# Turned attention tiles: mirrored by the fetch in place of the store

## The chip, the cores and the metric

The kernel runs on 1 core of one Trainium2 chip. The metric is the device time of one execution in microseconds (us); the three times of the kernel before are 1122.34, 1119.64 and 1121.96, their median is 1121.96 us.

## The reference, cut to what matters

```python
# 2 batches, S = 3136, D = 256, d_qk = 64, d_ff = 1024, float32
scores = (1 / S) * (z @ z.T)              # per batch, symmetric
attn   = maximum(scores, 0) ** 2          # symmetric too
x      = u * (attn @ v)
h      = maximum(x @ w_in, 0)
conv   = depthwise convolution of h over 3 neighbouring rows, conv_w
x      = (h * sigmoid(conv)) @ w_out
xn     = (x - mean) / sqrt(var + 1e-6) * g_ln
out    = x + maximum(xn @ w_ch1, 0) @ w_ch2
```

## The kernel before

**Tiling.** A batch's 3136 columns (queries) are cut into 7 chunks of 4, 4, 3, 4, 3, 3 and 4 tiles of 128, so a chunk is 512, 384 or (the last, with a half tile) 448 wide. Its rows (keys) are 25 tiles `j` of 128. For a chunk `c` and a tile `j` the kernel needs the squared scores `a`, 128 keys by the chunk's queries. `products` computes them: two matmuls, a Relu on ACT, a square on ACT or DVE. `scores` then splits `a` into a rounded part `ah` (ACT, sometimes DVE) and the rest `al` (DVE), and `av` adds six matmuls of both parts with `vh` and `vl` into PSUM.

**The mirror.** The matrix is symmetric, so a tile above the diagonal is the transpose of one below. For each tile whose keys belong to a later chunk, `spill` turns `a` on DVE (L624): the instruction transposes each block of 32 x 32 in its place, into a buffer `bl` (4 places). The blocks then still have to be exchanged. The kernel before does that in the store: four DMAs (two for the half tile), each of 32 partitions, write to the DRAM tensor `turned` in runs of 32 numbers, 128 bytes (L633). When the later chunk comes, `land` fetches its part of `turned` in one DMA, whole rows of 1.5 to 2 KB (L646), in place of the two matmuls and the square. There are 146 spills, 73 in each batch, mostly in the first chunks of a batch, and 154 fetches, mostly in the last ones. A fetch goes into one of the six places of `a`; at most four fetches hold places at once.

**The feed-forward blocks.** 17 blocks of 384 or 256 rows (`mlps`) run interleaved with attention, each when its chunks of `x` are through DRAM. Weights are loaded and decoded on DVE and ACT during the first chunks.

**Order.** All of this is a list of operations with the engines that may do them, prices (`PRICE`), due times and buffers. `Program.order` simulates the five queues (PE, ACT, DVE, POOL and SP, which issues every DMA) and emits the operations in the order of that simulation; each engine then runs its own queue in that order. A DMA books time of SP, and a transfer: `kb / RATE` in one shared pipe, then `LANDS`. Where the plan has a gap on PE, `fill` (L1128) puts matmuls of zeros. The old spill books 1.92 us of SP and `kb=w`, the old fetch 0.45 us and `kb=n/2`, for `w` or `n` columns.

Of the kernel before, what the change touches and what calls it, by code (L numbers as in the profile page):

```python
# [8 lines left out]
F32 = mybir.dt.float32  # L9
# [6 lines left out]
P = 128  # L16
NB, S, D, DQ, DFF = 2, 3136, 256, 64, 1024
# [5 lines left out]
TILES = [4, 4, 3, 4, 3, 3, 4]  # L23
SQ = 32
# [24 lines left out]


PRICE = {
    "mm": lambda n: 0.0087 + 0.000431 * n,
    "turn": lambda n: 0.109,
    "act": lambda n: 0.06 + 0.0009 * n,
    "pool_u32": lambda n: 0.2 + 0.0013 * n,
# [12 lines left out]
}  # L68

AFTER = {"PE": 0.2, "ACT": 0.165, "DVE": 0.15, "POOL": 0.13, "SP": 0.0}  # L70
RATE, LANDS = 300.0, 1.9
ENGINES = ("PE", "ACT", "DVE", "POOL", "SP")


# [15 lines left out]
class Program:  # L90
# [7 lines left out]
    def op(self, ways, fn, reads=(), writes=(), adds=(), takes=(), due=None, late=None, name="", port=False, kb=None):  # L98


        o = Op()
        o.ways, o.fn, o.due, o.late, o.name, o.port, o.kb = ways, fn, due, late, name, port, kb
        o.before, o.after, o.n = set(), [], len(self.ops)
        o.adds, o.spare = tuple(adds), None
        for k in reads:
            assert k in self.writers, (name, k)
            o.before.update(self.writers[k])
            self.readers.setdefault(k, []).append(o)
        for k in writes:
            o.before.update(self.writers.get(k, ()))  # L110
            o.before.update(self.readers.pop(k, ()))
            self.writers[k] = [o]
        for k in adds:
            o.before.update(self.readers.get(k, ()))
            self.writers.setdefault(k, []).append(o)
        o.before.discard(o)
        bufs = []
        for k in (*reads, *writes, *adds, *((t,) for t in takes)):
            if isinstance(k[0], Buf) and k[0] not in bufs:
                bufs.append(k[0])  # L120
        for b in bufs:
            b.users.append(o)
        o.bufs = bufs
        self.ops.append(o)
        return o
# [168 lines left out]
def attn_moe_kernel(ctx: ExitStack, tc: tile.TileContext, zt, ut, v, w_in, conv_w, w_out, g_ln, w1, w2, out):  # L294
    nc = tc.nc
# [9 lines left out]
    dram = ctx.enter_context(tc.tile_pool(name="dram", bufs=1, space=bass.MemoryType.DRAM))  # L305
# [63 lines left out]
    op = pr.op  # L369
    orders = {}  # L370

    def buf(tag, fixed=False, kind=None):
        if fixed:
            orders[tag] = orders.get(tag, 0) + 1
        return Buf(tag, orders[tag] if fixed else None, kind)

    def at(b, name=None):

        if b.ap is None:
            b.ap = tags[b.tag][1](name or b.tag)  # L380
        return b.ap
# [3 lines left out]
    def price(kind, n):  # L385
        return PRICE[kind](n)
# [213 lines left out]
    per = len(TILES)  # L600
    start_of = [sum(TILES[:i]) for i in range(per + 1)]
# [11 lines left out]
    turned = {}  # L613
    for c in range(NC):
        i = c % per
        rows = S - start_of[i + 1] * P
        if rows > 0:
            turned[c] = dram.tile([P * TILES[i], rows], F32, tag=f"turned{c}", name="turned")

    def spill(c, j, ab):  # L620
        w = chunks[c][1] - chunks[c][0]
        b = buf("bl")
        op(
            [("DVE", price("dve_turn", w))], lambda e: nc.vector.transpose(at(b, "bl")[:, :w], at(ab)[:, :w]),  # L624
            reads=[(ab, 0)], writes=[(b, 0)], name="bl", port=True,
        )
        k0 = (j - start_of[c % per + 1]) * P

        def write(e):
            blocks_ = at(b)[:, :w].rearrange("p (b k) -> p b k", k=SQ)  # L630
            for o in range(0, min(P, S - j * P), SQ):
                dst = turned[c][:, k0 + o : k0 + o + SQ].rearrange("(b q) k -> q b k", q=SQ)
                nc.sync.dma_start(out=dst, in_=blocks_[o : o + SQ])  # L633

        op([("SP", 1.92)], write, reads=[(b, 0)], writes=[("turned", c, j)], late=LANDS + w / RATE, kb=w, due=1e4, name="spill")

    def land(c, j):
        q0, q1 = chunks[c]
        n, i = q1 - q0, chunk_of[j]
        src = c - c % per + i  # L640
        k0 = (start_of[c % per] - start_of[i + 1]) * P
        r0 = (j - start_of[i]) * P
        b = buf("a", True, kind="ld")
        op(
            [("SP", 0.45)],
            lambda e: nc.sync.dma_start(out=at(b, "land")[:, :n], in_=turned[src][r0 : r0 + P, k0 : k0 + n]),  # L646
            late=LANDS + n / 2 / RATE, kb=n / 2, writes=[(b, 0)], name="land",
            reads=[("turned", src, jj) for jj in range(start_of[c % per], start_of[c % per + 1])],
        )
        return b  # L650

    def scores(c, j, due):
        q0, q1 = chunks[c]
        n = q1 - q0
        from_dram = mirrored(c, j)
        ab = land(c, j) if from_dram else buf("a", True)

        def a():
# [9 lines left out]
        if spilled(c, j):  # L668
            spill(c, j, ab)
# [468 lines left out]
    for o in order:  # L1138
# [8 lines left out]
        n = int((gaps.get(o, 0.0) - 0.1) / FILL)  # L1147
# [5 lines left out]
    for i in list(nc.cur_bb.bb.instructions):  # L1153
        e = str(i.engine)
# [47 lines left out]
```

## Time and profile before

| | |
|---|---|
| median of three times | 1121.96 us |
| span of the profiled execution (its own total isn't given) | 1119.3 us |
| PE busy | 1098.5 us (98%) |
| DVE busy | 857.9 us (77%) |
| ACT busy | 714.5 us (64%) |
| granted TensorE clock | 1.000 |
| DMA queue q1 | 326960 packets, 114.21 MB, 42.2% of 16 engines |
| packets under 512 bytes | 276528 |
| stores `turned<-bl` | 560 issues (372 of 64 KB, 188 of 48 KB) |
| fetches `land<-turned` | 154 issues (82 of 192 KB, 42 of 224 KB, 30 of 256 KB) |

A busy time is the union of an engine's instructions; matmuls are pipelined, so a busy PE may still be waiting inside. "SPq" is the queue of SP, whose issues aren't counted as busy. Releasers are inferred from semaphores.

### The profile page before, as it was taken

Reading aid. Unit: us, or ns where it says so; the run is one execution under the profiler, and the core shown is the slowest. Engines: PE = TensorE matmul, PEld = TensorE weight load, DVE = VectorE, ACT = ScalarE, POOL = GpSimd, SP = SyncE. Lnnn points to the kernel's source line nnn. Section 1 sums busy time; section 2 is a strip of 40 time slices with the busy share of each in tenths; the row PEclk is TensorE's granted clock in tenths of the full one; section 3 lists DMA queues with packets and bytes.
Section 4 is the critical chain, followed back from the end, with each engine's and each line's share of the span. In section 5 each row is a group of like instructions: output and inputs, shape, how many; then the busy total and the mean of one; then the engine's idle time right before and its main releaser. Section 6 shows DMA issues by size and latency. Waiting matters only on the chain.

```text
span 1119.3 us, 18987 instructions
## 1 busy us (share of the span) xinstructions
PE 1098.5 (98%) x6686; PEld 1028.0 (92%) x6686; DVE 857.9 (77%) x1810; ACT 714.5 (64%) x1473; POOL 30.4 (3%) x43
## 2 busy tenths in 40 slices
PE   9899999999999999999999999999999999999998
PEld 7777787899999989999999999999999999999998
DVE  7888889989869686868687778785857868477773
ACT  7668767786647576757665666664737647366552
POOL 2000000000000000000000000000000000000000
PEclk9999999999999999999999999999999999999999
DMA  7788877975444224253316242412433524220000
GB/s 199 149 199 157 198 148 181 225 179 175 96 126 134 76 64 81 43 90 83 70 44 109 83 78 63 103 50 51 90 109 92 146 65 122 76 82 27 25 15 19
DMA packets 327054, 115.41 MB, mean 103 GB/s; under 512 B 276528, under 2 KB 314800, under 8 KB 326960
## 3 DMA queue, kind: packets, MB, share of 16 engines
q1 hardware_dynamic: 326960, 114.21, 42.2%
q8 instruction: 52, 0.85, 0.3%
q14 instruction: 42, 0.34, 0.1%
HBM read 64.74 MB, written 46.47 MB: 99 GB/s over the span
## 4 chain that ended last, share of the span: by engine, by line
PE 85%; DVE 4%; DMA 4%; ACT 4%; issue 1%; SPq 1%; POOL 0%; DVEq 0%; ACTq 0%
PE av L739 10%; PE av L736 10%; PE av L738 10%; PE y L839 8%; PE y L837 8%; PE y L838 8%; PE h2ps L821 4%; PE h2ps L822 4%; PE h2ps L823 4%; PE hps L821 4%; PE hps L822 4%; PE hps L823 4%; PE s L694 3%; PE s L695 3%; DMA land<-turned 2%; DVE al L673 2%
## 5 line engine op out<-in xcount | busy, mean ns | idle before, releaser
L736 PE MATMUL av<-ah,vh 128*128 128x512 f32 (+2 forms) x700 | 258.5, 369 | 5.1 <-ACT ah L393 2.3
L739 PE MATMUL av<-ah,vl 128*128 128x512 f32 (+2 forms) x700 | 256.0, 366 | 0.0
L738 PE MATMUL av<-al,vh 128*128 128x384 f32 (+2 forms) x672 | 248.3, 370 | 6.6 <-DVE al L673 6.1
L1015 DVE SCALAR_TENSOR_TENSOR g2l<-h2ps,g2h 128x384 fp32r<-128x384 f32 (+1 forms) x136 | 73.2, 539 | 125.1 <-ACT g2h L1010 124.4
L1010 ACT ACTIVATE g2h<-h2ps 128x384 fp32r<-128x384 f32 (+1 forms) x136 | 65.1, 479 | 146.2 <-PE h2ps L823 145.5
L736 PEld LDWEIGHTS av<-ah,vh 128*128 128x128 f32 x700 | 131.7, 188 | 19.8 <-ACT ah L393 5.0
L738 PEld LDWEIGHTS av<-al,vh 128*128 128x128 f32 x672 | 126.4, 188 | 23.2 <-DVE al L673 13.2
L739 PEld LDWEIGHTS av<-ah,vl 128*128 128x128 f32 x700 | 131.6, 188 | 14.1
L703 ACT ACTIVATE a<-s 128x512 f32<-128x512 f32 (+2 forms) x196 | 105.9, 558 | 45.5 <-PE s L695 45.1
L673 DVE TENSOR_TENSOR al<-a,ah 128x512 fp32r<-128x512 f32 (+2 forms) x182 | 114.2, 637 | 9.2 <-ACT ah L393 8.5
L837 PE MATMUL y<-woh,gh 128*128 128x256 f32 x392 | 109.7, 280 | 0.7 <-DVE ysb L1023 0.7
L839 PE MATMUL y<-woh,gl 128*128 128x256 f32 x392 | 109.9, 280 | 0.3 <-DVE gl L903 0.3
L837 PE MATMUL y<-w2h,g2h 128*128 128x256 f32 x392 | 109.8, 280 | 0.2 <-DVE ysb L1023 0.2
L624 DVE STREAM_TRANSPOSE bl<-a 128x512 f32<-128x512 f32 (+1 forms) x146 | 95.0, 657 | 19.4 <-ACT a L712 9.9
L839 PE MATMUL y<-w2h,g2l 128*128 128x256 f32 x392 | 109.8, 280 | 0.0
L838 PE MATMUL y<-w2l,g2h 128*128 128x256 f32 x392 | 109.7, 280 | 0.0
L838 PE MATMUL y<-wol,gh 128*128 128x256 f32 x392 | 109.6, 280 | 0.0
L393 ACT CAST ah<-a 128x512 fp32r<-128x512 f32 (+2 forms) x185 | 105.8, 583 | 4.4 <-DVE a L708 3.2
L712 ACT ACTIVATE a<-a 128x512 f32<-128x512 f32 (+2 forms) x183 | 105.9, 593 | 1.4
L673 DVE TENSOR_TENSOR al<-land,ah 128x384 fp32r<-128x384 f32 (+2 forms) x154 | 90.3, 595 | 16.5 <-ACT ah L393 15.8
L863 ACT ACTIVATE t<-h,cw 128x384 f32<-128x384 f32 (+1 forms) x136 | 81.9, 605 | 27.8 <-DVE gl L903 26.6
L393 ACT CAST ah<-land 128x384 fp32r<-128x384 f32 (+2 forms) x146 | 78.5, 547 | 31.5 <-DMA land<-turned 22.4
(119 smaller groups left out, 2442.9 us busy)
## 6 DMA issues: line engine op xcount, KB each, us to landing
turned<-bl SPq DMA_DIRECT2D x372, 64.0 KB, 1.9
land<-turned SPq DMA_DIRECT2D x82, 192.0 KB, 3.1
land<-turned SPq DMA_DIRECT2D x42, 224.0 KB, 3.9
turned<-bl SPq DMA_DIRECT2D x188, 48.0 KB, 1.8
land<-turned SPq DMA_DIRECT2D x30, 256.0 KB, 3.4
out_dram<-ysb SPq DMA_DIRECT2D x15, 384.0 KB, 2.8
vst<-in_v_dram SPq DMA_DIRECT2D x11, 512.0 KB, 4.0
x<-gated SPq DMA_DIRECT2D x14, 386.0 KB, 3.8
```

The costliest lines, as they stand in the source:

```text
L393: nc.scalar.copy(dst, src)
L624: [("DVE", price("dve_turn", w))], lambda e: nc.vector.transpose(at(b, "bl")[:, :w], at(ab)[:, :w]),
L673: lambda e: nc.vector.tensor_tensor(at(al, "al")[:, :n], a(), f(at(ah)[:, :n]), ALU.subtract),
L703: [("ACT", price("act_ps", n))], lambda e: nc.scalar.activation(a(), at(ps)[:, :n], AF.Relu),
L712: op([("ACT", price("act", n))], lambda e: nc.scalar.activation(a(), a(), AF.Square), writes=[(ab, 0)], name="square")
L736: nc.tensor.matmul(p, vhj, at(ah)[:, :n], start=first(b, d), stop=False, **kw)
L738: nc.tensor.matmul(p, vhj, at(al)[:, :n], start=False, stop=False, **kw)
L739: nc.tensor.matmul(p, vlj, at(ah)[:, :n], start=False, stop=False, **kw)
L821: nc.tensor.matmul(p, a, h_, start=d == 0, stop=False)
L837: nc.tensor.matmul(p, a, wh, start=first(acc, (i0 + i) // 2), stop=False, **kw)
L838: nc.tensor.matmul(p, a, wl, start=False, stop=False, **kw)
L839: nc.tensor.matmul(p, b, wh, start=False, stop=k == NF - 1, **kw)
```

## The change

The store writes `bl` as it stands, 128 partitions in one DMA, to a tensor of another shape: one plane of 128 columns for each tile of the chunk, in runs of 128 numbers (512 bytes). The fetch exchanges the blocks: four DMAs, each to 32 partitions, in runs of 32 numbers (128 bytes). The planner's prices of both follow, so do `LANDS` (1.9 to 1.6) and the price of a matmul, and all orders are planned anew with them. Number and shapes of the operations on PE, ACT, DVE and POOL stay, but for the fillers.

```diff
-    "mm": lambda n: 0.0087 + 0.000431 * n,
+    "mm": lambda n: 0.0022 + 0.000449 * n,
...
-RATE, LANDS = 300.0, 1.9
+RATE, LANDS = 300.0, 1.6
+SPILL_KB, LAND_KB = 0.53, 0.91
...
-        rows = S - start_of[i + 1] * P
-        if rows > 0:
-            turned[c] = dram.tile([P * TILES[i], rows], F32, tag=f"turned{c}", name="turned")
+        later = sum(TILES[i + 1 :])
+        if later > 0:
+            turned[c] = dram.tile([TILES[i], later * P, P], F32, tag=f"turned{c}", name="turned")
...
-        k0 = (j - start_of[c % per + 1]) * P
+        r0 = (j - start_of[c % per + 1]) * P
+        rows = min(P, S - j * P)
         def write(e):
-            blocks_ = at(b)[:, :w].rearrange("p (b k) -> p b k", k=SQ)
-            for o in range(0, min(P, S - j * P), SQ):
-                dst = turned[c][:, k0 + o : k0 + o + SQ].rearrange("(b q) k -> q b k", q=SQ)
-                nc.sync.dma_start(out=dst, in_=blocks_[o : o + SQ])
-        op([("SP", 1.92)], write, reads=[(b, 0)], writes=[("turned", c, j)], late=LANDS + w / RATE, kb=w, due=1e4, name="spill")
+            dst = turned[c][:, r0 : r0 + rows, :].rearrange("t p x -> p t x")
+            nc.sync.dma_start(out=dst, in_=at(b)[:rows, :w].rearrange("p (t x) -> p t x", x=P))
+        op(
+            [("SP", 0.4)], write, reads=[(b, 0)], writes=[("turned", c, j)],
+            late=LANDS + SPILL_KB * w / RATE, kb=SPILL_KB * w, due=1e4, name="spill",
+        )
...
-        k0 = (start_of[c % per] - start_of[i + 1]) * P
-        r0 = (j - start_of[i]) * P
+        g0 = (start_of[c % per] - start_of[i + 1]) * (P // SQ)
         b = buf("a", True, kind="ld")
-        op(
-            [("SP", 0.45)],
-            lambda e: nc.sync.dma_start(out=at(b, "land")[:, :n], in_=turned[src][r0 : r0 + P, k0 : k0 + n]),
-            late=LANDS + n / 2 / RATE, kb=n / 2, writes=[(b, 0)], name="land",
+        def read(e):
+            blocks_ = turned[src][j - start_of[i]].rearrange("(g q) (b k) -> b q g k", q=SQ, k=SQ)
+            for o in range(P // SQ):
+                nc.sync.dma_start(
+                    out=at(b, "land")[o * SQ : (o + 1) * SQ, :n].rearrange("p (g k) -> p g k", k=SQ),
+                    in_=blocks_[o, :, g0 : g0 + n // SQ, :],
+                )
+        op(
+            [("SP", 1.92)], read, late=LANDS + LAND_KB * n / RATE, kb=LAND_KB * n, writes=[(b, 0)], name="land",
             reads=[("turned", src, jj) for jj in range(start_of[c % per], start_of[c % per + 1])],
         )
```

## Rows read from the trace of the kernel before

**Rows 1.** Busy time of each engine by stretch; then granted clock, DMA share, GB/s.
```profile
40.00:160.00 120.00, 110.58 (x531) 91.84 (x529) 99.21 (x189) 87.29 (x180) 3.33 (x4) 1.00 0.83 174
160.00:320.00 160.00, 157.28 (x895) 146.18 (x896) 143.54 (x301) 116.07 (x239) 3.22 (x4) 1.00 0.66 171
320.00:1008.00 688.00, 686.80 (x4281) 654.66 (x4281) 505.55 (x1069) 423.61 (x863) 13.87 (x14) 1.00 0.34 83
...
180.00:200.00 20.00, 20.00 (x94) 16.55 (x93) 19.68 (x38) 17.55 (x36) 0.00 (x0) 1.00 0.74 161
```

**Rows 2.** The same of the fillers' line L1128 alone, PE and PEld.
```profile
40.00:160.00 120.00, 5.86 (x41) 5.72 (x41) 1.00 0.83 174
```

**Rows 3.** Chain of waits, pieces (start us, us, what); its lines, 40 to 160.
```profile
23.93 0.72 PE warm_ps L1128 x6
...
by line: DMA turned<-bl 13.0%; SPq L633 10.0%; DMA land<-turned 9.8%; DVE al L673 8.9%; issue 8.3%; ACT ah L393 8.2%; ACT a L712 6.5%; ACT a L703 5.7%; DVE bl L624 4.5%; PE av L739 3.6%; PE av L738 3.5%; PE av L736 3.3%; DMA zst<-in_zt_dram
...
45.52 0.49 SPq L633
...
47.88 2.00 DMA turned<-bl
```

**Rows 4.** Timeline of SP: start us, us, line, what is issued, count.
```profile
86.47 6.50 SPq L633 DMA_DIRECT2D turned<-bl  x12
...
97.30 13.13 SPq L633 DMA_DIRECT2D turned<-bl  x24
...
216.24 0.57 SPq L760 DMA_DIRECT2D gated<-u  x1
```

**Rows 5.** Waits of SP's queue, 40 to 160: us in total, times, longest.
```profile
SPq L633 <- DVE al L673: 1.9, 5, 0.5
...
SPq L576 <- PE av L739: 0.5, 1, 0.5
```

**Rows 6.** Instructions of `turned` and `bl`, 40 to 160, then 200 to 320 (ns min/median/max).
```profile
L633 SPq DMA_DIRECT2D turned<-bl x163: 302/490/1785, 39.9 to 159.8; - x163
L646 SPq DMA_DIRECT2D land<-turned x12: 319/440/2162, 73.2 to 156.8; - x12
...
L624 DVE STREAM_TRANSPOSE bl<-a x41: 535/703/715, 40.6 to 156.8; 128x512 f32<-128x512 f32 x28, 128x384 f32<-128x384 f32 x13
...
L633 SPq DMA_DIRECT2D turned<-bl x57: 303/468/798, 199.5 to 309.0; - x57
L646 SPq DMA_DIRECT2D land<-turned x44: 320/413/987, 203.4 to 318.7; - x44
```

**Rows 7.** Waits of the engines, 40 to 160; the last row 160 to 320.
```profile
ACT ah L393 <- DMA land<-turned: 11.0, 6, 3.2
...
DVE bl L624 <- DMA turned<-bl: 6.3, 5, 2.6
...
PE av L738 <- DVE al L673: 4.5, 6, 2.0
...
ACT ah L393 <- DMA land<-turned: 7.6, 8, 3.2
```

**Rows 8.** DMA issues, 200 to 320: KB each, median us to landing.
```profile
land<-turned SPq DMA_DIRECT2D x33, 192.0 KB, 3.4
wst<-in_w_dram SPq DMA_DIRECT2D x5, 512.0 KB, 5.1
...
turned<-bl SPq DMA_DIRECT2D x40, 48.0 KB, 2.3
...
gated<-u SPq DMA_DIRECT2D x2, 384.0 KB, 3.8
...
lh<-hl SPq DMA_DIRECT2D x2, 96.0 KB, 2.5
```

**Rows 9.** DMA queue: packets, MB, share of 16 engines; 423 to 431, then 978 to 998.
```profile
q1 hardware_dynamic: 7543, 0.94, 70.6%
...
q1 hardware_dynamic: 1515, 2.38, 40.9%
```

## The prediction

> **What bounds the kernel now.** I first read the busy shares of the page, then the same engines stretch by stretch. Over the span PE is busy 1098.5 of 1119.3 us, at full granted clock, so PE bounds the program as a whole, and time can be won only where PE does nothing useful. [rows 1] has the three stretches that decide. From 320 to 1008 us PE is idle 1.2 us of 688: nothing is to be had. From 40 to 160 us it is idle 120 - 110.58 = 9.4 us, and 41 of its matmuls there are fillers, which the planner puts where it foresees a gap [rows 2]. Six cost 0.72 us in the chain [rows 3], so 41 cost 41 x 0.12 = 4.9 us. That makes 9.4 + 4.9 = 14.3 us of PE time without useful work. From 160 to 320 us PE is idle for 2.7 us.
>
> Next I asked what holds PE back from 40 to 160 us. It is not the arithmetic alone: DVE has 99.2 and ACT 87.3 us of 120 [rows 1]. SP's timeline shows it [rows 4]: 24 quarter-stores of turned tiles in 13.13 us without a break, 12 in 6.50 us. All of SP's waits in the stretch add up to 7.4 us (seven rows, the first and the last in [rows 5]), so SP is occupied 112.6 of 120 us: by 163 quarter-stores, 12 fetches and some 20 others. An issue takes 0.49 us (median; up to 1.79) [rows 6], and with the step to the next one 13.13 / 24 = 0.55 us. The chain of waits says the same from the other side: "DMA turned<-bl" 13.0%, "SPq L633" 10.0% and "DMA land<-turned" 9.8% make a third of it there [rows 3]. Its pieces at 45 and 47 us are an issue and then a landing, with PE and DVE waiting at their end. In the list of waits ACT waits 11.0 us for fetches and DVE 6.3 us for stores to free a place of `bl` [rows 7]. Behind either stands an engine's whole in-order queue, and at its end PE's `av` waits for `al`.
>
> **The change, part by part.** *Stores.* A turned tile takes one issue in place of four (two for a half tile). From 40 to 160 us there are 41 turns [rows 6], so 163 issues become 41: 122 fewer, 67 us less of SP. No row shows the new store's issue. Its bounds are 0.30 us (the shortest quarter-store [rows 6]) and 4 x 0.49 = 1.96 us (if the time went by the rows moved). The nearest row is `gated<-u`, a store of all partitions: 0.57 us [rows 4]; I take 0.55. For the transfer, a stretch with nothing but quarter-stores has 7543 packets in 70.6% of 16 engines over 8 us: 12.0 ns for 128 bytes. One with nothing but fetches moves 2.38 MB in 40.9% of 16 engines over 20 us: 55 ns for 1000 bytes [rows 9]. A run of 512 bytes lies between 12 and 48 ns; at the fetches' rate it is 28 ns, which I take. A 512-wide store then costs the engines 512 x 28 / 16 = 0.9 us in place of 2048 x 12 / 16 = 1.5 us. A place of `bl` is held for four issues and a landing now, 2.2 + 2.3 = 4.5 us; then for one issue and a landing of some 3 us (2.3 for a quarter, 3.8 for `gated<-u` [rows 8]), 3.6 us.
>
> *Fetches.* One issue becomes four of 32 partitions, the shape of a quarter-store, so I take 0.55 us each; the bounds are 0.32 and 0.99 us, the shortest and the longest fetch issue from 200 to 320 us [rows 6]. From 40 to 160 us 12 fetches add 36 issues, 20 us. SP then needs 112.6 - 67 + 20 = 66 of 120 us and stops setting the pace. A fetch's last piece is issued 3 x 0.55 = 1.65 us after the first and lands, if it does as a quarter-store, 2.3 us later: 3.95 us against 3.4 now [rows 8]. Bounds: 0 later (its pieces share the engines with nothing) to 2 us later (3.8 us as for `gated<-u`). Four places, filled ahead, cover that. The engines take 1536 x 12 / 16 = 1.15 us for a 384-wide fetch, in place of 197 KB x 55 / 16 = 0.7 us.
>
> *What the front gains.* At most 14.3 us, when PE works there without a gap; at least 0, when another engine takes over at once (below 0 only if the store gets dearer to issue, case C). The same work in 105.7 us asks DVE for 99.2, or 94%. DVE can do that: from 180 to 200 us it is busy 19.68 of 20 with PE at 20.00 [rows 1]. But the decoding of weights, which lies in this stretch, leaves little cover. I take two thirds, 9.5 us.
>
> *What the middle loses.* From 200 to 320 us there are 44 fetches, 57 quarter-stores (15 tiles) [rows 6] and 25 others (12 rows, the first and the last in [rows 8]). They become 176 + 15 + 25 = 216 issues, 119 of 120 us: SP's full stretch moves there. The backlog of feed-forward work covers it: from 160 to 320 us PE is busy 157.3 of 160 [rows 1] although ACT waits 7.6 us for fetches [rows 7]. Bounds: 0 (the backlog covers all) to 14.3 us (what a full SP costs at the front). I take 2.7 us, as much again as PE is idle there now. After 320 us some 90 of the 154 fetches are left on 688 us, 198 us of issue; PE has its backlog, and I take 0.
>
> *Prices of the planner.* The matmul price goes from 0.229 to 0.232 us at 512 columns, from 0.1742 to 0.1746 at 384 and from 0.119 to 0.117 at 256, so other orders come out also where no store lies. PE's idle time outside the two stretches is 20.8 (span less busy time) - 9.4 - 2.7 = 8.7 us. New orders can move it either way; bounds -3 and +3, a third of it, taken as 0.
>
> *The sum.* -9.5 + 2.7 = -6.8 us. Of the profiled execution the span is given, 1119.3 us, and the three times lie 0.3 to 3.0 us above it. I put the difference on the median: 1121.96 - 6.8 = **1115.2 us**. The forecast's own range is 1105 (14.3 and the middle's 2.7 won) to 1118.6.
>
> *A rule of the Trainium skill.* The rows: a quarter-store of 48 KB lands in 2.3 us, a fetch of 192 KB in 3.4 [rows 8], and each issue takes 0.55 us of SP. "DMA: Bandwidth & Descriptors", Rules for kernel authors, tells to coalesce many small transfers into one, since under 64 KB one pays mostly overhead. That speaks for the new store and against the new fetch, whose pieces have 48 to 64 KB; by it alone the fetches lose what the stores gain, and the sum is about 0. The trace agrees in so far as issues fill SP at the front.
>
> **The rivals.** *A: arithmetic takes over.* SP is free, but DVE's in-order queue (turns, splits, decoding) holds PE from 40 to 160 us as before. For it: PE's longest wait there is for DVE's `al`, 4.5 us [rows 7], and DVE is at 83%. Against: DVE reaches 98% right behind, with PE full. The gain is 3 us, eaten by the middle's 2.7: 1122.
>
> *B, slower: the queue emptied at the front fills in the middle.* Place: SP from 200 to 320 us. It decides when SP's need passes 120 us, and 119 is reckoned; single issues take up to 1.79 us [rows 6], and ten of those would do. A late fetch stands ahead of all later issues of SP, its `ah` stops ACT, and PE reaches `av` without it. Price: what a full SP costs at the front, 14.3 us, so 1121.96 - 9.5 + 14.3 = 1126.8. For it: the count above, and the 11.0 us that ACT waits for 12 fetches where SP is full. Against: the plan now books 1.92 us of SP for a fetch and can put feed-forward work in between.
>
> *C: the store is no cheaper to issue.* At 1.96 us SP saves 9 us by the stores (163 x 0.55 - 41 x 1.96) and pays 20 for fetches: 124 of 120 us at the front, some 4 us late, with the front's stall as now and the middle fuller than in B: 1121.96 + 4 + 14.3 = 1140. `gated<-u` speaks against it.
>
> **How the numbers follow.** Forecast 0.60, A 0.17, B 0.19, C 0.04. The three times differ by 0.24%; I count 0.3%, 3.4 us, as a difference. So faster (below 1118.6) is 0.60, same 0.17, slower 0.23. The range leaves out C: from 1103 (14.3 and 2.7 won, and 2 of the orders' 3 us) to 1128 (B and 1 us of the orders).
>
> **What would show it.** Right: from 40 to 160 us SP's timeline has gaps, with some 110 issues; PE is idle under 5 us with few fillers; "SPq" and "DMA turned<-bl" are nearly gone from the chain there. From 200 to 320 us SP is full, and ACT waits over 10 us for `land` while PE's idle time stays under 6 us. Packets under 512 bytes stay about as many, now of fetches. Wrong: if PE stands idle 9 us at the front with DVE or ACT as the releaser (A), if its idle time from 160 to 320 us passes 12 us (B), or if the new store takes over 1 us to issue (C).

## The result, and the profile after

The changed kernel takes 1109.56 us (median of 4 runs, 1107.01 to 1110.30) against 1121.59 us for the kernel before (4 runs, 1119.64 to 1122.34). The ratio is 0.9889, with a 95% interval from 0.9875 to 0.9904: 1.1% faster. The profiled span goes from 1119.3 to 1107.2 us.

First the stretches, as in [rows 1], now of the changed kernel; then the fillers (L1138 here) from 40 to 160 and from 160 to 320 us, as in [rows 2].

```profile
40.00:160.00 120.00, 118.63 (x579) 102.58 (x578) 113.78 (x219) 98.59 (x202) 2.96 (x6) 1.00 0.74 192
160.00:320.00 160.00, 157.72 (x931) 148.27 (x930) 134.83 (x287) 103.72 (x215) 5.04 (x5) 1.00 0.73 157
320.00:1008.00 688.00, 686.19 (x4263) 653.49 (x4262) 515.44 (x1097) 427.17 (x866) 13.43 (x14) 1.00 0.36 82
...
40.00:160.00 120.00, 2.19 (x13) 2.03 (x13) 1.00 0.74 192
160.00:320.00 160.00, 3.87 (x25) 3.55 (x25) 1.00 0.73 157
```

From 40 to 160 us PE's idle time fell from 9.4 to 1.4 us and its fillers from 41 to 13, so it did 579 - 13 = 566 useful matmuls there in place of 531 - 41 = 490. DVE rose from 99 to 114 us of 120. From 160 to 320 us PE is idle for 2.3 us, nearly as before (2.7), but there are 25 fillers in place of 8.

The stores and fetches from 40 to 160 us, the chain of waits there, ACT's wait for fetches from 40 to 160 and from 160 to 320 us, and SP's longest wait from 40 to 160 us answer to [rows 6, 3, 7, 5]:

```profile
L651 SPq DMA_DIRECT2D land<-turned x68: 320/489/1973, 58.7 to 159.4; - x68
L634 SPq DMA_DIRECT2D turned<-bl x42: 359/377/1089, 41.2 to 156.4; - x42
...
by line: PE av L746 18.5%; PE av L749 18.3%; PE av L748 17.9%; DMA x<-gated 6.2%; PE s L705 5.1%; PE s L704 5.1%; ACT a L713 3.5%; issue 2.7%; ACT ah L394 2.4%; ACT a L722 2.3%; DVE al L683 2.2%; DVE bl L626 1.5%; PE hps L831 1.3%; ACT L897
...
ACT ah L394 <- DMA land<-turned: 2.0, 2, 1.1
...
ACT ah L394 <- DMA land<-turned: 13.8, 9, 2.4
...
SPq L634 <- DVE bl L626: 16.8, 20, 1.7
```

The stores' issues and landings, 23% of the chain before, are gone from its head, and the matmuls are there. ACT's wait for fetches went from 11.0 to 2.0 us at the front (40 to 160 us) and from 7.6 to 13.8 us in the middle (160 to 320 us). All of SP's waits from 40 to 160 us add up to 55.1 us now, so SP is occupied 64.9 of 120 us; from 200 to 320 us they add up to 14.2 us, so it is occupied 105.8. That is where SP is full now, as its timeline from 240 us on shows (start, us, what, count):

```profile
240.02 12.57 SPq L651 DMA_DIRECT2D land<-turned  x22
252.69 0.56 SPq L770 DMA_DIRECT2D gated<-u  x1
253.36 2.28 SPq L651 DMA_DIRECT2D land<-turned  x4
...
262.59 14.30 SPq L651 DMA_DIRECT2D land<-turned  x20
```

The two kernels run their matmuls in different orders, so a stretch of time doesn't compare the same work. For that I add up, over the records of the matmuls in order of their start, the columns that each one streams, fillers left out. Every kernel here has 2,328,928 in all. The table gives the time at which a number of columns is reached, for the kernel before, and the difference from it for each other kernel of this study (minus is earlier). The last column is the span of the profiled execution:

```
columns, thousands    150     350     650    1750    2250    span
before, us           91.4   193.3   334.0   841.6  1077.9  1119.3
changed              -9.6   -18.9   -13.4   -14.1   -12.7   -12.1
e1 four issues       -1.8    +6.0   +19.4   +20.3   +24.1   +24.3
e2 short runs        -5.7   -10.1    +1.1    +1.0    +2.5    +3.0
e3 old orders        -6.8   -16.2    +2.7    +6.3   +20.6   +20.6
e4 prices only       +3.0    +5.0    +4.2    +4.0    +4.8    +4.8
e5 one fetch         -9.3   -18.6   -18.4   -19.3   -17.8   -17.4
e6 booked 2.3        -9.3   -18.8   -18.2   -17.9   -19.2   -19.1
e7 mixed, 3 to 6     +1.0    -6.7    -5.4    -5.3    -4.0    -3.6
e8 mixed, all        +1.2    -8.7    -7.5    -7.0    -5.6    -5.5
e9 before, booked    -6.5    -5.5    -6.0    -5.8    -5.9    -5.4
e10 booked 2.15     -10.8   -17.5   -17.0   -16.3   -15.1   -15.1
e11 booked 2.5      -10.6   -19.6   -14.7   -12.6   -11.0   -10.5
e12 old mm price     -9.9   -16.8   -12.5   -11.0    -8.6    -8.3
```

Each row is of one profiled execution; those of e3 and e7 are some 4 us slower than the median of their kernel. The changed kernel wins 18.9 us up to 193 us of the kernel before, gives 5.5 back up to 334 us, and another 1.3 on the rest of the way.

### The profile page after: what moved, and what is told of

Read it like the earlier page. It is cut to its first block, busy times and chain, and to the rows that moved or that the text cites. A ratio compares the mean times of both kernels' runs of the same rounds, so it can differ in the third digit from the quotient of the medians.

```text
span 1107.2 us, 19228 instructions
## 1 busy us (share of the span) xinstructions
PE 1093.4 (99%) x6674; PEld 1027.3 (93%) x6674; DVE 863.4 (78%) x1828; ACT 705.2 (64%) x1452; POOL 31.4 (3%) x46
## 4 chain that ended last, share of the span: by engine, by line
PE 87%; DVE 4%; DMA 3%; ACT 3%; SPq 2%; issue 1%; POOL 0%; DVEq 0%; ACTq 0%
PE av L746 11%; PE av L749 11%; PE av L748 11%; PE y L847 8%; PE y L849 8%; PE y L848 8%; PE h2ps L831 4%; PE h2ps L832 4%; PE h2ps L833 4%; PE hps L831 4%; PE hps L832 4%; PE hps L833 4%; PE s L704 3%; PE s L705 3%; DMA land<-turned 2%; SPq L651 1%
## 5 line engine op out<-in xcount | busy, mean ns | idle before, releaser
L749 PEld LDWEIGHTS av<-ah,vl 128*128 128x128 f32 x700 | 131.7, 188 | 14.3
L394 ACT CAST ah<-land 128x384 fp32r<-128x384 f32 (+2 forms) x136 | 73.8, 546 | 34.7 <-DMA land<-turned 16.7
L882 DVE SCALAR_TENSOR_TENSOR t<-h,cw,t 128x384 f32<-128x384 f32 (+1 forms) x136 | 80.7, 598 | 14.6 <-ACT t L873 14.1
```

Source lines behind the costliest of these rows:

```text
L394: nc.scalar.copy(dst, src)
L749: nc.tensor.matmul(p, vlj, at(ah)[:, :n], start=False, stop=False, **kw)
```

## The experiments

Times are medians beside the kernel before on the same chip; ratios are to it, with 95% intervals.

**e1: the number of issues alone.** The changed kernel and its orders; only the store is cut.

```diff
-            nc.sync.dma_start(out=dst, in_=at(b)[:rows, :w].rearrange("p (t x) -> p t x", x=P))
+            src = at(b)[:rows, :w].rearrange("p (t x) -> p t x", x=P)
+            for o in range(0, rows, SQ):
+                nc.sync.dma_start(out=dst[o : o + SQ], in_=src[o : o + SQ])
```

> The changed kernel with its orders kept, but each store of a turned tile goes out as four issues of 32 partitions again, still in 512-byte runs. Theory 1 (the front was held by the number of issues on SP): the front stretch, 40 to 160 us, then needs some 42 x 4 + 68 + 20 = 256 issues, over 120 us of SP at 0.55 us each, so SP is full again and the time goes back to 1118 to 1135 us, with SPq in the chain of the front. Theory 2 (it was held by the DMA engines, busy with 128-byte runs): the runs are long, so the time stays at 1108 to 1112 us.

1145.7 us, ratio 1.0212 [1.0192, 1.0232], above the range of theory 1. The gain is gone, and more. From 40 to 160 us, the stretch's row, its stores and fetches, and the chain:

```profile
40.00:160.00 120.00, 107.67 (x478) 88.46 (x477) 95.92 (x182) 82.74 (x170) 3.54 (x7) 0.96 0.65 165
...
L636 SPq DMA_DIRECT2D turned<-bl x154: 302/430/1550, 39.9 to 159.9; - x154
L653 SPq DMA_DIRECT2D land<-turned x48: 373/468/1662, 69.3 to 158.8; - x48
...
by line: DMA turned<-bl 11.4%; DMA land<-turned 10.6%; SPq L636 9.0%; DVE al L685 6.8%; SPq L653 6.6%; issue 5.0%; DMA x<-gated 4.3%; DMA wst<-in_w_in_dram 3.6%; PE av L750 2.9%; ACT a L724 2.9%; ACT ah L394 2.8%; DVE a L720 2.7%; DVE bl L6
```

The DMA engines are busy 65% of the stretch, less than in any other kernel here, with the stores in 512-byte runs; yet PE is idle for 12.3 us (9.4 before), SP is occupied 106.1 of 120 us (its waits add up to 13.9) and the stores' landings and issues head the chain again. Theory 2 falls for this stretch: the issues suffice to bring the loss back. How much they cost is overstated here, for two reasons. The orders book 0.4 us of SP for a store that now takes four issues. And the granted clock is 0.96 there, and 0.992 over the span: PE waited 4.3 us for the square on DVE, and then 3.4 us ran at 1.2 GHz, the lower of the clock's two levels (row below; the upper is 2.4 GHz); over the span the clock costs 0.8% of 1143.6, up to 9 us.

```profile
56.00:59.40 3.40, 3.40 (x10) 2.63 (x9) 3.40 (x7) 3.40 (x8) 0.00 (x0) 0.50 0.72 183
```

**e2: the runs alone.** Orders kept, one issue for a store, in runs of 128 bytes.

```diff
-turned[c] = dram.tile([TILES[i], later * P, P], F32, ...)
+turned[c] = dram.tile([TILES[i], P // SQ, later * P, SQ], F32, ...)
-dst = turned[c][:, r0 : r0 + rows, :].rearrange("t p x -> p t x")
+dst = turned[c][:, :, r0 : r0 + rows, :].rearrange("t b p k -> p (t b) k")
...
-blocks_ = turned[src][j - start_of[i]].rearrange("(g q) (b k) -> b q g k", q=SQ, k=SQ)
+blocks_ = turned[src][j - start_of[i]].rearrange("b (g q) k -> b q g k", q=SQ)
```

> The changed kernel with its orders kept and one issue for each store, but in 128-byte runs (the tensor in memory is laid out so that each run of 32 numbers stands alone; the fetch reads the same runs as before). Theory 1 (issues on SP): 1108 to 1113 us, DMA share of the front back at 0.8 or more. Theory 2 (128-byte runs on the DMA engines): 1116 to 1122 us. If an issue's time goes by the runs that it describes (2048 in place of 512), the store's issue takes some 1.5 to 2 us and the time is 1115 us or more by theory 1 too; the issue's own duration tells.

1124.5 us, ratio 1.0025 [1.0013, 1.0038]: all of the gain is lost again, against theory 1 and a little beyond the range of theory 2. The DMA queue and the issues from 40 to 160 us show what happened:

```profile
q1 hardware_dynamic: 108961, 21.65, 100.5%
...
L651 SPq DMA_DIRECT2D land<-turned x59: 321/481/3078, 63.9 to 159.7; - x59
L634 SPq DMA_DIRECT2D turned<-bl x42: 359/810/3956, 39.4 to 152.9; - x42
```

With short runs on both sides the 16 engines are busy all the time. The shortest issue of a 512-wide store still takes 0.36 us, in 2048 runs as in 512, so its time doesn't go by the number of runs. But in the median it takes 0.81 us and at most 3.96, against 0.38 and 1.09 in the changed kernel, where the engines are busy 74%: SP's 124 issues in the stretch take 94 us, the changed kernel's 136 take 70. That full engines hold the issue up is the likely reason; no run shows it apart. Half of the front's gain stays (-10.1 us at 350 thousand), the rest and the middle are lost. So there are two limits at the front: issues (e1), and the engine time of 128-byte runs, which binds when both sides have them. Whether the 83% of the kernel before, with short runs in the stores alone, cost it anything is not shown. The change lowers both.

**e3: new transfers, orders of before.** All prices are those of the kernel before, so is every queue's order.

```diff
-        op([("SP", 0.4)], write, ..., late=LANDS + SPILL_KB * w / RATE, kb=SPILL_KB * w, due=1e4, name="spill")
+        op([("SP", 1.92)], write, ..., late=LANDS + w / RATE, kb=w, due=1e4, name="spill")
-        op([("SP", 1.92)], read, late=LANDS + LAND_KB * n / RATE, kb=LAND_KB * n, ..., name="land")
+        op([("SP", 0.45)], read, late=LANDS + n / 2 / RATE, kb=n / 2, ..., name="land")
```

> The new store and the new fetch under all the old prices, so every engine has the order of the kernel before. Theory 1: the waits for SP at the front go, though the fillers stay; the fetches cost more SP time than the order has booked, so part is lost in the middle: 1110 to 1117 us. Theory 3 (the new orders bring the gain, not the transfers): 1120 us or more.

1138.0 us, ratio 1.0145 [1.0115, 1.0174]: the number is that of theory 3, the course is not. The front's gain comes with the transfers alone, -16.2 us at 350 thousand columns. Then orders that book 0.45 us for a fetch of four issues lose 18.9 us in the middle and 14 us more between 1750 and 2250 thousand columns, where the second batch fetches; some of that is the clock, 0.97 in the middle. So the transfers bring most of the front's gain, and the new orders keep it from being lost again. PE's row and ACT's wait from 160 to 320 us:

```profile
160.00:320.00 160.00, 148.76 (x813) 135.83 (x812) 128.10 (x269) 102.57 (x212) 1.73 (x2) 0.97 0.70 151
...
ACT ah L394 <- DMA land<-turned: 29.7, 18, 4.0
```

**e4: prices only.** The kernel before with `"mm": 0.0022 + 0.000449 * n` and `LANDS = 1.6`.

> The kernel before with the new price of a matmul and LANDS of 1.6 alone; stores and fetches as before. Theory 1: 1118 to 1124 us, the front's SP as full as before. Theory 3 (the price of a matmul and the orders that follow bring the gain): 1108 to 1113 us.

1126.0 us, ratio 1.0040 [1.0027, 1.0052], 2 us above the range of theory 1. PE is still idle for 10.8 us from 40 to 160 us, and the granted clock is 0.96 there:

```profile
40.00:160.00 120.00, 109.16 (x505) 90.98 (x504) 97.24 (x182) 81.10 (x165) 3.46 (x5) 0.96 0.80 168
```

That costs 4% of 120, some 5 us of full speed, as much as the two profiled spans differ by (1124.1 and 1119.3 us). The clock isn't all of it, though: an execution of e4 with a clock of 0.999 took 1124.75 us. Either way the new prices alone bring no gain, and theory 3 in its first form (the matmul price) is out.

**e5: the fetch in one issue.** Orders kept. The fetch takes the same bytes, in whole rows, and leaves out the exchange of the 32 x 32 blocks, so this kernel computes something else; it is there for its time alone.

```diff
-            for o in range(P // SQ):
-                nc.sync.dma_start(out=at(b, "land")[o * SQ : (o + 1) * SQ, :n]..., in_=blocks_[o, :, g0 : g0 + n // SQ, :])
+            plane = turned[src][j - start_of[i]].rearrange("r x -> (r x)")[g0 * SQ * P : (g0 * SQ + n) * P]
+            nc.sync.dma_start(out=at(b, "land")[:, :n], in_=plane.rearrange("(p m) -> p m", p=P))
```

> The changed kernel with its orders kept; each fetch takes the same bytes in one issue of 128 partitions, in whole rows, and leaves the exchange of the 32 x 32 blocks out, so that part of the computation is changed. If the middle's loss (18.9 us ahead of the kernel before at 193 us, 13.5 us at 334 us) comes from the fetches' four issues on SP and their short runs: SP has over 40% free from 160 to 320 us, ACT waits under 5 us for land there (13.8 now), and the time is 1101 to 1106 us. If the loss is in the orders (25 fillers are planned at 200 to 240 us) or in DVE and ACT: 1107 to 1111 us.

1103.2 us, ratio 0.9828 [0.9814, 0.9843]. With the same orders the middle loses 0.2 us in place of 5.5 (table), and PE's idle time from 160 to 320 us goes to 0.1 us. Both have the same 25 fillers. So the give-back is the fetch's issues and runs, not the fillers. Which of the two, e5 doesn't say, since it changes both; SP's issues without a gap from 240 us on, with the engines busy 71% from 240 to 280 us, speak for the issues.

```profile
160.00:320.00 160.00, 159.90 (x968) 153.44 (x967) 139.08 (x297) 107.15 (x222) 5.08 (x5) 1.00 0.51 154
```

**e6, e10, e11: SP booked otherwise.** The changed kernel with a store at 0.45 us of SP and a fetch at 2.3 (e6), 2.15 (e10) and 2.5 us (e11), planned anew.

```diff
-            [("SP", 0.4)], write, ...
+            [("SP", 0.45)], write, ...
-            [("SP", 1.92)], read, ...
+            [("SP", 2.3)], read, ...
```

> The changed kernel, with SP booked nearer to what the trace shows: 2.3 us for a fetch (4 x 0.55 and a little; 1.92 in the changed kernel), 0.45 us for a store (0.40). All orders are planned anew. If the middle's loss comes from orders that ask for more of SP than it gives, ACT's wait for land from 160 to 320 us goes down to some 8 us and the time to 1104 to 1108 us. If SP's need itself is the limit there: 1107 to 1112 us.

> The changed kernel with a fetch booked at 2.15 us of SP (2.3 in the run before it, 1.92 in the changed kernel) and 0.45 for a store. If the booking is what counts: 1100 to 1105 us. If the 1101.2 us of 2.3 was a lucky order: 1105 to 1112 us.

> The same with 2.5 us for a fetch, more than it takes. If the booking counts, the stretch is booked somewhat too long and fillers take the place of waits: 1101 to 1107 us. If 2.3 was a lucky order: 1105 to 1112 us.

1101.2 us (0.9813 [0.9799, 0.9828]), 1106.3 (0.9860 [0.9836, 0.9884]) and 1111.2 (0.9899 [0.9881, 0.9917]). e6 is below the range expected and beats both kernels of the diff. Its row of the middle and ACT's wait there:

```profile
160.00:320.00 160.00, 159.06 (x957) 151.22 (x956) 138.47 (x293) 106.02 (x216) 5.79 (x6) 1.00 0.71 156
...
ACT ah L394 <- DMA land<-turned: 6.9, 9, 2.3
```

All three have the front's gain (-17.5 to -19.6 us). The middle then loses 0.6, 0.5 and 4.9 us, so the two bookings near the trace (four issues at 0.57 us, the pace of the 22 shown from 240 us on, are 2.3 us) keep it, and the longer one doesn't, as 1.92 doesn't (5.5 us in the changed kernel, 4.3 in e12). With one plan for each booking that is a hint, not shown. e10 and e11 lose 2 to 4 us more, spread over the rest. So the two came out where a lucky order was expected, and part of e6's lead is that: the same transfers under five plans that book the fetch's four issues (these, the changed kernel and e12) take 1101 to 1113 us. The old transfers under three plans (the kernel before, e4 and e9) take 1116 to 1126 us, so the two groups don't overlap.

**e7, e8: mirrored by the store for the first chunk.** In the first batch, the first chunk's tiles for chunks 3 to 6 (e7), or all of its tiles (e8), go the old way, the rest the new way. The core:

```diff
+    def by_store(src, dst):      # e7; e8 without the condition on d
+        b, s = divmod(src, per)
+        d = dst % per
+        return b == 0 and s == 0 and d >= 3
...
+        if by_store(c, c - c % per + chunk_of[j]):   # store and fetch of the kernel before, its prices
```

> A mixture: the first chunk's tiles that the chunks 3 to 6 of the first batch will fetch are mirrored by the store (four issues, one for the fetch), all others by the fetch. That moves 3 issues of each of 14 tiles out of the stretch from 150 to 390 us into the first 60 us, where SP has room, and takes some 48 issues out of the middle. If SP's need limits the middle: 1103 to 1107 us. If the front's DMA engines or bl's places don't bear the stores: 1108 to 1113 us.

> The same mixture for all 21 stored tiles of the first chunk of the first batch. By the count of issues alone it frees SP most in the middle: 1102 to 1107 us. But the first 60 us then have 63 more issues, and 128-byte runs on the DMA engines; if the front is as tight as the run with short runs showed, it loses there: 1108 to 1116 us.

1113.7 us (0.9926 [0.9900, 0.9952]) and 1115.8 us (0.9943 [0.9926, 0.9960]): better than before, worse than the changed kernel, and so the second of the two outcomes expected (e7 a little above its range). The middle gives back only about 1 us, but the front's first part is as slow as before (+1.0 and +1.2 us at 150 thousand columns). SP's timeline of e8 there has the picture of [rows 4] again, and from 40 to 80 us PE is busy 35.39 us (34.33 before, 39.15 in the changed kernel):

```profile
43.94 6.50 SPq L644 DMA_DIRECT2D flipped<-bl  x11
50.54 0.45 SPq L418 DMA_DIRECT2D zst<-in_zt_dram  x1
51.03 4.73 SPq L644 DMA_DIRECT2D flipped<-bl  x8
55.87 0.92 SPq L543 DMA_DIRECT2D wst<-in_w_in_dram  x2
56.88 9.39 SPq L644 DMA_DIRECT2D flipped<-bl  x12
...
40.00:80.00 40.00, 35.39 (x161) 28.63 (x160) 31.32 (x57) 22.97 (x44) 1.28 (x2) 0.96 0.81 166
```

**e9: the kernel before, booked better.** A store's four issues at 2.3 us in place of 1.92, transfers as they were.

> The kernel before with its transfers kept and SP booked nearer to the trace: 2.3 us for a store's four issues in place of 1.92; orders planned anew. If the front was slow only because its order asked too much of SP: 1105 to 1112 us, as for the changed kernel. If SP's issues themselves were the limit at the front (occupied 112.6 of 120 us): 1117 to 1124 us, with SP still full from 40 to 160 us.

1116.2 us, ratio 0.9948 [0.9932, 0.9964], between the two: about 6 of the front's 19 us could be had from the order alone, with SP as full as before (its waits from 40 to 160 us add up to 13.2 us; 12.5 before). No run shows the rest without fewer issues; other bookings of the old transfers were not tried.

**e12: the old matmul price.** The changed kernel with `"mm": 0.0087 + 0.000431 * n`.

> The changed kernel with the old price of a matmul, orders planned anew. If the matmul price has no part in the gain, as the run with prices only suggests: 1106 to 1113 us. If the plan needs it: 1114 us or more.

1112.6 us, ratio 0.9912 [0.9893, 0.9930], as expected if the price has no part in the gain: in the scatter of the orders, with the front's gain (-16.8 us).

## Why the prediction was right, and where it was off

The forecast was faster, 1115.2 us in a range from 1103 to 1128; measured was 1109.56. The mechanism is as said: SP's issues held the front (e1), and the change moved them to the middle (e5). Two terms of the sum were too small. Their errors partly cancel, so part of how near the sum came is luck: -18.9 + 5.5 + 1.3 = -12.1 us of span were measured for -6.8.

*What the front gains* was set at 9.5 us and at most 14.3. Measured: 18.9 us by 193 us. The bound was wrong, since it took PE's busy time at its word. A matmul of 512 columns is shown for 0.40 us while the next one starts after 0.23, so a wait can hide some 0.17 us under a busy PE. Counted in columns, the changed kernel is 0.4 us ahead where the kernel before is at 40 us, and 16.0 us where that is at 160: 15.6 us in the stretch, where idle time and fillers show 8.0 + 28 x 0.12 = 11.4. The 4.2 us between would be 25 waits of 0.17 us, an estimate that fits the starts of the matmuls: against the pace of an unbroken run, 39 of them came over 0.03 us late in this stretch before, and 14 do now. The stretch also reached on to 193 us, which brought 2.9 us more. And the caution behind the two thirds was needless: DVE went to 113.8 of 120 us, 95%, and PE's idle time to 1.4. That speaks against rival A.

*What the middle loses* was set at 2.7 us. Measured: 5.5, shown by e5 to be the fetch. The signs came as named: ACT waits 13.8 us, PE stands idle 2.3 us. Rival B had the place right and its price, 14.3 us, not: e3 has that price (18.9 us), but under orders that don't know of the fetch's four issues. So B's counter-argument, that the plan books them, held; the old matmul price, which e3 has too, costs no such thing (e12).

*The store's issue* takes 0.377 us in the median, near its lower bound, for 0.55; case C is out. *A place of `bl`* is held for 0.38 us of issue and 2.4 to 2.8 us until the landing, some 3 us for 3.6 reckoned. *The engines' time* went the way that was said: DMA share at the front fell from 0.83 to 0.74 although more work was done. *SP's occupation* at the front was overstated: the seven rows added up for 7.4 us were the longest of 21, which add up to 12.5 us, so it was occupied 107.5 of 120 us. That it needs 64.9 us now, for 66 reckoned, is partly luck: the store's issue is cheaper than reckoned, and there are 68 fetch issues in the stretch where 48 were. *The orders* were set at -3 to +3 us outside the two stretches; behind 334 us the five plans with the same transfers give from -0.9 to +4.2 us, and over the whole span they differ by 11 us. So this bound was too narrow, and 1109.56 is one draw of them.

## What to carry to other kernels

When one queue issues every DMA, count its issues per stretch; the same exchange costs four issues on whichever side does it, so put it on the side whose stretch has room, and book what an issue takes in the trace. Estimate what a stall costs from the columns that the matmuls got done, not from PE's busy time. Where a planner makes the orders, compare several plans with and without an edit before one per cent is put down to it: here one edit under five plans spread over 11 us.

## What had not been expected of the hardware

At the front a store of 128 partitions in 512-byte runs was issued in 0.38 us in the median (0.36 at the least), faster than a quarter of it in 128-byte runs before (0.49 in the median, 0.30 at the least), and one in 2048 runs of 128 bytes also takes 0.36 us at the least; its median passed 0.8 us only where the engines were full (e2). And idle time of PE cost more than itself: in e1, e3 and e4 stretches of 3.4 us at 1.2 GHz followed waits of PE of 0.9 to 4.3 us, and three of them make the 5 us of full speed that e4 lost from 40 to 160 us. In the profiled execution of the kernel before the clock is 1.00 in every row shown, though PE waited for up to 2.0 us [rows 7]; others of its executions have a mean of down to 0.995.
